# Attention with its maxima in a fused pre-LN block: seven PSUM banks shared by score and maximum products, each bank named in a fixed order, and most exponentials over one bank

## The chip, the cores and the metric

The kernel runs on one core of a Trainium2 chip, in one launch. The time is device microseconds from the first to the last instruction and what lies around them, the median of several runs. Engines are called as in the profile: PE (matrix products; PEld is its loading of weights), DVE (vector), ACT (activation), POOL, and SP, which issues most of the DMAs.

## The reference

S = 2048 rows, D = 512, 32 heads of 16. An attention block with a residual, then a gated MLP with a 2048x2048 mixing matrix and a residual. The change lies in the attention alone:

```
h  = x + attention(layernorm(x), wqkv, wo)
       scores = einsum("bhqd,bhkd->bhqk", q, k) * 16 ** -0.5
       p      = softmax(scores, axis=-1)
       o      = einsum("bhqk,bhkd->bhqd", p, v)
h2 = h + gmlp(layernorm(h), w_in, w_sp, b_sp, w_out)
```

## The kernel before

The kernel has four stages: layer norm and the projections to q, k and v; the attention; the first half of the MLP; the product with the mixing matrix and the output. The attention is worked in **units** (hg, qb, kb): four heads, 512 queries, 128 keys, 512 units in all. The loop takes two units per turn, and this text calls such a turn a **step**. What a step holds:

- Eight **score products** (L709), one per head and unit: 128 keys by 512 queries, contracted over 50 rows. A head is held in its own half of the rows of PE (t = 0 in rows 0 to 49, t = 1 in rows 64 to 113), so two products of different t can be in PE together. In the 50 rows are three pieces of q and k and two rows that subtract the row's maximum.
- Four **exponentials** (L715) on ACT, each over two banks of PSUM, 128x1024, into an SBUF tile `pt`.
- The **weighted sums** (L726), `pv`: four products of 32 columns side by side, over 512 queries (letter V) or over 256 (letter h, twice per unit).
- One **maximum step** for a group of queries eleven steps ahead: eight products over 48 rows (L235) into banks of their own. Six are read by a `reduce_max` on DVE (L240; letters M and m, four with t = 1 and two with t = 0). For the other two, keys were combined ahead: one (v) is read by an `abs` on ACT (L245), the other (u) by DVE, together with the result of that `abs` (L249).

The order on PE, ACT, DVE and SP is written by hand, as lists of letters that `play` reads (`ORDER` for six steps of eight, `FIRST_TWO` for the first two steps of 512 queries, `START` for the very first). An S in the list is a score product, and every second S issues the exponential too; a letter with a number is a product of the maximum step and the bank that it goes to. N, T and G set the ends of groups: negated maxima, their turning into rows, and the copy of the finished `pv` by ACT (L734). Semaphores are not written by hand: the tile framework puts a wait on an instruction where its tiles ask for one.

PSUM is cut into eight tiles of one bank (128x512 f32 each): `pv` one, `m0` to `m2` three (pool `ps_m`), and two tiles `s` of two banks (pool `ps_s`). A tile `s` gets two products and is read by one exponential; the two tiles alternate. Steps with maxima are those with n // 2 + 11 < 256, so 245 of them. In the last eleven, `FOUR` and plain code set the order, and a third tile `s` takes the place of the banks of the maxima.

## Time and profile before

| what | value |
|---|---|
| median of 3 runs | 1850.18 us (1849.63 to 1851.09) |
| profiled execution, span from first to last instruction | 1848.2 us |
| what lies around the span (median less span) | 2.0 us |
| ACT busy, `abs` in 300 to 1200 us | 186 times, so 186 steps in 900 us: 4.84 us each |
| PE's weight loads waiting for DVE to read a bank of maxima, 300 to 1300 us | 286.5 us, 568 times |
| granted PE clock | 1.00 in every stage but the end |

In the profile, a row of the view in order of time gives start, duration, engine, line, operation and tiles, then a count, and in brackets how long the engine had been idle and what ended that. Of PE two kinds of row are shown, its weight loads (PEld) and its matmuls; a matmul cannot start before its load, and it is the load that waits for a semaphore.

### The profile page before, as it was taken

How to read it: one execution, taken by the hardware profiler on the slowest of the kernel's cores; microseconds unless marked ns; L12 is line 12 of the kernel's file. 1: busy time of each engine (PE TensorE's matmuls, PEld its weight loads, DVE VectorE, ACT ScalarE, POOL GpSimd, SP SyncE). 2: the span in 40 equal slices, each digit the busy share in tenths (PEclk: the TensorE clock that was granted, in tenths of full speed). 3: DMA queues.
4: the chain of work that ended last, by engine and by line, in shares of the span. 5: the costliest groups of instructions: out<-in, count | busy, mean ns of one | idle time of the engine just before them, and what ended most of it. 6: DMA issues, size and time to landing. Idle time of an engine off the chain costs nothing.

```text
span 1848.2 us, 35986 instructions
## 1 busy us (share of the span) xinstructions
PE 1840.2 (100%) x13362; PEld 1028.3 (56%) x13362; DVE 1519.0 (82%) x3030; ACT 1363.4 (74%) x1696; POOL 225.7 (12%) x305
## 2 busy tenths in 40 slices
PE   9999999999999999999999999999999999999999
PEld 6875334433334333344333334343437889999998
DVE  6578999999999999999999999999936766877664
ACT  3325999999999999999999999999995444434221
POOL 2241000011010100000000000000001756001111
PEclk9999999999999999999999999999999999999999
DMA  6778111221120111022011012100124555768662
GB/s 195 198 193 193 42 25 31 55 47 29 39 57 18 53 39 25 17 50 39 14 39 38 19 30 49 25 14 14 31 55 124 165 162 170 224 189 272 200 195 91
DMA packets 148759, 160.15 MB, mean 87 GB/s; under 512 B 63096, under 2 KB 93320, under 8 KB 147240
## 3 DMA queue, kind: packets, MB, share of 16 engines
q1 hardware_dynamic: 143800, 146.44, 29.5%
q10 hardware_dynamic: 4752, 11.41, 1.6%
q8 instruction: 105, 1.72, 0.4%
q14 instruction: 70, 0.57, 0.1%
q0 software_dynamic: 32, 0.01, 0.0%
HBM read 101.26 MB, written 55.61 MB: 85 GB/s over the span
## 4 chain that ended last, share of the span: by engine, by line
PE 99%; DVE 0%; ACT 0%; issue 0%; DVEq 0%; ACTq 0%
PE pv L726 29%; PE m L235 22%; PE s L709 15%; PE acc L106 6%; PE acc L108 5%; PE acc L107 5%; PE g L108 4%; PE g L107 4%; PE g L106 4%; PE acc L644 2%; PE tp L1300 1%; PE acc L1321 0%; PE tp L996 0%; PE tp L389 0%; PE h L644 0%; PE acc L465 0%
## 5 line engine op out<-in xcount | busy, mean ns | idle before, releaser
L240 DVE TENSOR_REDUCE mx<-m 128x1 f32<-128x512 f32 x1508 | 948.5, 684 | 94.1 <-PE m L235 64.1
L715 ACT ACTIVATE pt<-s 128x1024 f32<-128x1024 f32 x1024 | 1012.5, 1024 | 12.6 <-PE m L235 6.6
L726 PE MATMUL pv<-pt,vst 128*32 128x256 f32 (+1 forms) x6048 | 590.5, 466 | 0.0
L235 PE MATMUL m<-kst,qst 48*128 48x512 f32 x1508 | 578.0, 468 | 0.1
L709 PE MATMUL s<-qst,kst 50*128 50x512 f32 x2048 | 568.1, 427 | 0.6 <-ACT pt L715 0.5
L235 PEld LDWEIGHTS m<-kst,qst 48*128 48x128 f32 x1508 | 236.7, 184 | 342.6 <-DVE mx L240 302.8
L709 PEld LDWEIGHTS s<-qst,kst 50*128 50x128 f32 x2048 | 273.5, 184 | 136.4 <-ACT pt L715 92.2
L726 PEld LDWEIGHTS pv<-pt,vst 128*32 128x32 f32 x6048 | 122.8, 108 | 227.5 <-issue 215.4
L235 PE MATMUL m<-uvs,qst 48*128 48x512 f32 x497 | 227.7, 458 | 0.0
L245 ACT ACTIVATE ab<-m 128x512 f32<-128x512 f32 x248 | 148.4, 598 | 76.5 <-PE m L235 76.4
L249 DVE CUSTOM_DVE_ANT_0 ab<-m,ab 128x512 f32<-128x512 f32 x249 | 169.4, 680 | 10.6 <-ACT pt L715 9.9
L100 POOL CAST mparts<-nm 128x16 fp32r<-128x16 f32 x32 | 6.3, 198 | 881.7 <-DVE nm L253 881.7
L235 PEld LDWEIGHTS m<-uvs,qst 48*128 48x128 f32 x497 | 90.8, 183 | 37.5 <-DVE mx L240 37.5
L936 ACT ACTIVATE ws<-a 128x512 fp32r<-128x512 f32 x80 | 45.7, 621 | 48.7 <-PE g L108 23.9
L1015 ACT ACTIVATE z<-acc 128x464 f32<-128x464 f32 (+2 forms) x64 | 27.6, 456 | 67.1 <-PE acc L108 67.1
L106 PE MATMUL acc<-wi,hT 128*128 128x464 f32 (+2 forms) x196 | 72.8, 371 | 0.0
L108 PE MATMUL acc<-wi,hT 128*128 128x464 f32 (+2 forms) x196 | 71.8, 366 | 0.0
L107 PE MATMUL acc<-wi,hT 128*128 128x464 f32 (+2 forms) x196 | 71.6, 365 | 0.0
L937 DVE TENSOR_TENSOR ws<-a,ws 128x512 fp32r<-128x512 f32 x80 | 56.3, 746 | 11.6 <-ACT ws L936 11.4
L98 ACT ACTIVATE part<-acc 128x512 fp32r<-128x512 f32 x32 | 19.1, 597 | 60.9 <-PE acc L108 51.6
L106 PE MATMUL g<-b,ws 128*128 128x344 f32 x192 | 62.6, 326 | 0.0
L936 ACT ACTIVATE ws<-s 128x512 fp32r<-128x512 f32 x32 | 19.5, 631 | 57.7 <-DVE s L956 57.7
(201 smaller groups left out, 2156.9 us busy)
## 6 DMA issues: line engine op xcount, KB each, us to landing
a<-in_w_sp SPq DMA_DIRECT2D x80, 256.0 KB
qst<-q_scr SPq DMA_DIRECT2D x192, 64.0 KB
z_scr<-z ACTq DMA_DIRECT2D x32, 344.0 KB
kst<-k_scr SPq DMA_DIRECT2D x42, 256.0 KB
k_scr<-part SPq DMA_DIRECT2D x16, 512.0 KB
q_scr<-part SPq DMA_DIRECT2D x16, 512.0 KB
z<-z_scr SPq DMA_DIRECT2D x14, 344.0 KB
b<-z_scr SPq DMA_DIRECT2D x24, 172.0 KB
```

Of the source, the lines that this page charges most:

```text
L106: nc.tensor.matmul(ps, lh, rh, start=first, stop=False)
L107: nc.tensor.matmul(ps, lh, rl, start=False, stop=False)
L108: nc.tensor.matmul(ps, ll, rh, start=False, stop=last)
L235: nc.tensor.matmul(acc, q[r, p, c], keys[r, p], start=True, stop=True)
L240: nc.vector.reduce_max(at(t, e if t else e - 1), acc, axis=AX.X)
L245: nc.scalar.activation(ab[0], acc, AF.Abs)
L249: nc.vector.tensor_tensor_reduce(ab[0], acc, ab[0], 0.5, LOW, ALU.add, ALU.max, at(0, 0))
L709: nc.tensor.matmul(s[:, t, :], k[r, p, kb * P:(kb + 1) * P], q[r, p, :], start=True, stop=True)
L715: nc.scalar.activation(t, s, AF.Exp, scale=DH ** -0.5)
L726: nc.tensor.matmul(pv[0][32 * j:32 * j + 32, cols], vst[hg % 2][:, c:c + 32], pts[j % 2][:, j // 2, cols], start=kb == 0, stop=kb == NB - ...
L936: nc.scalar.activation(hi, src, AF.Copy)
L937: (nc.gpsimd if el == "pool" else nc.vector).tensor_sub(lo, src, hi.bitcast(F32))
```

## The change

One pool `ps_s` now holds one tile `s` of four banks, for all steps with maxima. Banks 3 to 6 in the lists are the four banks of that tile, banks 0 to 2 are still `m0` to `m2`. Score products and maximum products both go to any of the seven. In the lists, `Sa5` is a score product with t = 0 into bank 5, whose exponential (128x512, that one bank) is issued with it; `Sb1` has t = 1. A small s only makes the product; the exponential then follows the next big S and covers both banks (128x1024), through a slice of the tile `s` with a step from bank to bank. In ORDER all eight are single; in FIRST_TWO, now one list for two steps, four exponentials cover two banks and eight one. `pt` becomes three tiles of four banks' width in place of six of two, the same bytes. After the steps with maxima, a pool `ps_d` with two tiles `s` of two banks takes the place of the one of before, so the last eleven steps are as they were. The products, their number and their operands stay.

```
+MB = 3
-ORDER = "v2 S S M1 N S h m0 S m1 M2 S S h S M0 u1 T S V M0".split()
+ORDER = "Sa5 M6 m3 M2 v4 Sb1 h Sb6 u0 M5 Sa4 h Sb2 m3 Sb6 Sa1 N M4 Sa0 V T".split()
-START = "S S m1 M0 S S h M2 v1 S S m0 S S M2 u1 V M0".split()
-FIRST_TWO = ["v2 S S M1 S h S m2 M0 h G M1 S S m2 S m0 S V".split(),
-             "u2 S S M1 m0 S S h h v2 M1 S S M0 S S M2 u1 V M0".split()]
+START = "Sa5 M6 m3 M2 v4 Sb1 f Sb6 u0 M5 Sa4 Sb2 m3 Sb6 Sa1 M4 Sa0 V".split()
+FIRST_TWO = ("sa6 Sb5 M2 sa4 m1 Sb3 h M0 m2 Sa6 sb5 h G M0 v1 M3 Sa6 Sb4 u2 V v1 M0 m3 Sb5 u6 Sb2 "
+             "h Sa4 M1 Sa0 M5 h Sb6 sa4 Sb3 m2 M1 Sa0 V").split()
...
-        pp = at.enter_context(tc.tile_pool(name="pp", bufs=6))
+        pp = at.enter_context(tc.tile_pool(name="pp", bufs=3))
         ps_v = at.enter_context(tc.tile_pool(name="ps_v", bufs=1, space=PSUM))
-        ps_s = at.enter_context(tc.tile_pool(name="ps_s", bufs=2, space=PSUM))
+        singles = at.enter_context(ExitStack())
+        ps_s = singles.enter_context(tc.tile_pool(name="ps_s", bufs=1, space=PSUM))
...
+        def product(out, hg, qb, kb, t, p):
+            r = slice(RG * t, RG * t + KM)
+            nc.tensor.matmul(out, kst[hg % 2][r, p, kb * P:(kb + 1) * P], qst[hg * NQ + qb][r, p, :],
+                             start=True, stop=True)
+        def exp(out, scores):
+            nc.scalar.activation(out, scores, AF.Exp, scale=DH ** -0.5)
...
             for x in order:
-                if x == "S":
-                    if opened:
-                        pts.append(opened.pop()())
...
+                if x[0] in "sS":
+                    if not open_:
+                        open_.extend([units.pop(0), new_pt(), {}])
+                    unit, pt, places = open_
+                    t, b = "ab".index(x[1]), int(x[2:])
+                    p = sum(u == t for u, _ in places)
+                    out = bank(b)
+                    product(out, *unit, t, p)
+                    places[t, p] = len(places)
+                    made.append((b, out, (t, p)))
+                    if x[0] == "s":
+                        continue
+                    made.sort(key=lambda m: m[0])
+                    k = len(places) - len(made)
...
+                    if len(made) == 1:
+                        exp(pt[:, k, :], out)
                     else:
...
+                        b0, b1 = (m[0] - MB for m in made)
+                        exp(pt[:, k:k + 2, :], four[0][:, b0:b1 + 1:b1 - b0, :])
...
+        four.append(ps_s.tile([P, 4, 512], F32, name="s"))
+        for b in range(4):
+            more[MB + b] = lambda b=b: four[0][:, b, :]
...
                 if not steps and not later:
                     maxima.close()
+                    singles.close()
+                    doubles.append(at.enter_context(tc.tile_pool(name="ps_d", bufs=2, space=PSUM)))
```

What this makes of PE's queue is seen in a step of ORDER, the same step in both kernels. A row names the line, the products' output and inputs, and in brackets the engine whose semaphore the instruction waits for before it starts (`Activation_49` is ACT, `DVE_49` is DVE). First before, on PE, from the product v2 to m1; `s` is the tile of scores, `m` a bank of maxima, `pv` the weighted sum:

```order
L235 MATMUL m_10724<-uvs_106,qst 128x512
L709 MATMUL s<-qst,kst_105 128x512 [waits Activation_49]
L709 MATMUL s<-qst,kst_105 128x512
L235 MATMUL m_10733<-kst_105,qst 128x512 [waits DVE_49]
L709 MATMUL s<-qst,kst_105 128x512 [waits Activation_49]
L726 MATMUL pv<-pt,vst_103 32x256 x4
L235 MATMUL m_10742<-kst_105,qst 128x512 [waits DVE_49]
L709 MATMUL s<-qst,kst_105 128x512
L235 MATMUL m_10748<-kst_105,qst 128x512 [waits DVE_49]
```

Score products go to `s` alone and wait for ACT, one per tile of two banks; products into `m` wait for their reader. Now the same step after the change, on PE, from M2 to the second Sb6 of the list (M2, v4, Sb1, h, Sb6, u0, M5, Sa4, h, Sb2, m3, Sb6); L700 are score products, L236 products of the maximum step, and `s` is the tile of banks 3 to 6:

```order
L236 MATMUL m_10143<-kst_105,qst 128x512
L236 MATMUL s<-uvs_106,qst 128x512 [waits DVE_49]
L700 MATMUL m_10149<-qst,kst_105 128x512
L725 MATMUL pv<-pt,vst_103 32x256 x4
L700 MATMUL s<-qst,kst_105 128x512 [waits Activation_49]
L236 MATMUL m_10158<-uvs_106,qst 128x512
L236 MATMUL s<-kst_105,qst 128x512 [waits Activation_49]
L700 MATMUL s<-qst,kst_105 128x512 [waits DVE_49]
L725 MATMUL pv<-pt,vst_103 32x256 x4
L700 MATMUL m_10170<-qst,kst_105 128x512
L236 MATMUL s<-kst_105,qst 128x512 [waits Activation_49]
L700 MATMUL s<-qst,kst_105 128x512 [waits DVE_49]
```

Score and maximum products now alternate in the tile `s`; each of the six products into it carries a wait, and none of the four into `m` banks does in this stretch. The second place is FIRST_TWO, after the change, on PE (m2, Sa6 and sb5, h, M0, v1, M3, Sa6, Sb4, u2, V):

```order
L236 MATMUL m_10209<-kst_105,qst 128x512 [waits DVE_49]
L700 MATMUL s<-qst,kst_105 128x512 [waits Activation_49] x2
L725 MATMUL pv<-pt,vst_103 32x256 x4
L236 MATMUL m_10231<-kst_105,qst 128x512 [waits DVE_49]
L236 MATMUL m_10234<-uvs_106,qst 128x512
L236 MATMUL s<-kst_105,qst 128x512
L700 MATMUL s<-qst,kst_105 128x512 [waits DVE_49]
L700 MATMUL s<-qst,kst_105 128x512 [waits Activation_49]
L236 MATMUL m_10244<-uvs_106,qst 128x512
L725 MATMUL pv<-pt,vst_103 32x512 [waits PE_49]
```

Here half a weighted sum and the products M0 and v1 stand between sb5 and M3, and a whole weighted sum follows on Sb4 and u2; the products into `s` keep their waits except M3, ahead of which nothing has read `s` since sb5 was let in.

More of the change, by code (lines that the diff above doesn't have):

```diff
@@ L686, in block_kernel, with new_pt, score, weigh @@
         fixed(kst[1])
-        pp = at.enter_context(tc.tile_pool(name="pp", bufs=6))
+        pp = at.enter_context(tc.tile_pool(name="pp", bufs=3))
         ps_v = at.enter_context(tc.tile_pool(name="ps_v", bufs=1, space=PSUM))
-        ps_s = at.enter_context(tc.tile_pool(name="ps_s", bufs=2, space=PSUM))
+        singles = at.enter_context(ExitStack())
+        ps_s = singles.enter_context(tc.tile_pool(name="ps_s", bufs=1, space=PSUM))
         pv = {}
-        def score(*unit):
-            first, second = scores_of(*unit)
-            first()
-            return second()
-        def scores_of(hg, qb, kb, p):
-            q, k = qst[hg * NQ + qb], kst[hg % 2]
+        def new_pt():
+            return pp.tile([P, 4, 512], F32, name="pt")
+        def product(out, hg, qb, kb, t, p):
[4 more added lines that the diff above has]
+            nc.scalar.activation(out, scores, AF.Exp, scale=DH ** -0.5)
+        def score(unit, p, pt):
             turn[0] += len(later)
-            pool = later[0] if later and turn[0] % 3 == 2 else ps_s
+            pool = later[0] if turn[0] % 3 == 2 else doubles[0]
             s = pool.tile([P, 2, 512], F32, name="s")
-            def product(t):
-                r = slice(RG * t, RG * t + KM)
-                nc.tensor.matmul(s[:, t, :], k[r, p, kb * P:(kb + 1) * P], q[r, p, :],
-                                 start=True, stop=True)
             def second():
-                product(1)
-                t = pp.tile([P, 2, 512], F32, name="pt")
-                nc.scalar.activation(t, s, AF.Exp, scale=DH ** -0.5)
-                return t
-            return lambda: product(0), second
-        def weigh(hg, qb, kb, pts, cols=slice(0, 512)):
-            if kb == 0:
+                product(s[:, 1, :], *unit, 1, p)
+                exp(pt[:, 2 * p:2 * p + 2, :], s)
+            return lambda: product(s[:, 0, :], *unit, 0, p), second
+        def weigh(unit, pt, places, cols=slice(0, 512)):
+            hg, qb, kb = unit
+            if kb == 0 and cols.start == 0:
                 pv[0] = ps_v.tile([P, 512], F32, name="pv")
@@ L726, in weigh @@
                 nc.tensor.matmul(pv[0][32 * j:32 * j + 32, cols], vst[hg % 2][:, c:c + 32],
-                                 pts[j % 2][:, j // 2, cols], start=kb == 0,
+                                 pt[:, places[j // 2, j % 2], cols], start=kb == 0,
                                  stop=kb == NB - 1 and cols.stop == 512)
+        PLACES = {(t, p): 2 * p + t for t in range(2) for p in range(2)}
         def gather(hg, qb, pool=sm):
@@ L747, in gather, with play @@
             sums_[0] = (hg, cols, sums, pool)
-        def play(order, prev, unit):
-            hg, qb, *kbs = unit
+        def play(order, units):
             ending = pending[:]
@@ L754, in play @@
             ends.clear()
-            halves = [slice(0, 256), slice(256, 512)]
-            opened, pts = [], []
+            units = list(units)
+            open_, made = [], []
             for x in order:
-                if x == "S":
-                    if opened:
-                        pts.append(opened.pop()())
-                    else:
-                        k, p = divmod(len(pts), 2)
-                        first, second = scores_of(hg, qb, kbs[k], p)
-                        first()
-                        opened.append(second)
-                elif x == "h":
-                    cols = halves.pop(0)
-                    if prev is not None:
-                        weigh(*prev, cols)
-                    elif halves:
-                        pv[0] = ps_v.tile([P, 512], F32, name="pv")
-                        for j in range(4):
-                            nc.tensor.matmul(pv[0][32 * j:32 * j + 32, :], vst[0][:, :32],
-                                             vst[0][:, :512], start=True, stop=True)
+                if x[0] in "sS":
[12 more added lines that the diff above has]
+                    k = len(places) - len(made)
+                    for i, (_, _, head_) in enumerate(made):
+                        places[head_] = k + i
+                    if len(made) == 1:
+                        exp(pt[:, k, :], out)
+                    else:
+                        b0, b1 = (m[0] - MB for m in made)
+                        exp(pt[:, k:k + 2, :], four[0][:, b0:b1 + 1:b1 - b0, :])
+                    made.clear()
+                    if len(places) == 4:
+                        waiting.append([tuple(open_), 0])
+                        open_.clear()
+                elif x == "h":
+                    h = waiting[0][1]
+                    weigh(*waiting[0][0], slice(256 * h, 256 * h + 256))
+                    waiting[0][1] += 1
+                    if h:
+                        done[0] = waiting.pop(0)[0][0]
@@ L776, in play @@
                 elif x == "V":
-                    weigh(hg, qb, kbs[0], pts[:2])
+                    done[0] = waiting[0][0][0]
+                    weigh(*waiting.pop(0)[0])
                 elif x == "G":
-                    gather(*prev[:2])
+                    gather(*done[0][:2])
+                elif x == "f":
+                    pv[0] = ps_v.tile([P, 512], F32, name="pv")
+                    for j in range(4):
+                        nc.tensor.matmul(pv[0][32 * j:32 * j + 32, :], vst[0][:, :32],
+                                         vst[0][:, :512], start=True, stop=True)
@@ L785, in play @@
                         max_rows()
-                    elif kbs[0] == 6 and sums_:
+                    elif done[0] is not None and done[0][2] == 5 and sums_:
                         invert()
@@ L789, in play, with play_four @@
                     steps_of[x[0]].pop(0)(int(x[1:]))
-            assert not ending and len(pts) == 4
-            played.append(pts[2:])
-        def play_four(at, prev):
-            waiting, opened = [prev], []
+            assert not ending and not open_ and not units and not made
+        waiting, done, four, doubles = [], [None], [], []
+        def play_four(units):
+            opened, unit = [], None
             for x in FOUR:
@@ L798, in play_four @@
                     if opened:
-                        pts = waiting[-1][-1]
-                        pts.append(opened.pop()())
-                    else:
-                        if waiting[-1] is prev or len(waiting[-1][-1]) == 2:
-                            waiting.append((*at.pop(0), []))
-                        unit = waiting[-1]
-                        first, second = scores_of(*unit[:3], len(unit[-1]))
+                        opened.pop()()
+                        if p:
+                            waiting.append([(unit, pt, PLACES), 0])
+                            unit = None
+                    else:
+                        if unit is None:
+                            unit, pt, p = units.pop(0), new_pt(), -1
+                        p += 1
+                        first, second = score(unit, p, pt)
                         first()
@@ L808, in play_four @@
                 elif x == "V":
-                    unit = waiting.pop(0)
-                    weigh(*unit)
-                    if unit[2] == NB - 1:
-                        gather(*unit[:2])
+                    unit_ = waiting.pop(0)[0]
+                    weigh(*unit_)
+                    if unit_[0][2] == NB - 1:
+                        gather(*unit_[0][:2])
                 else:
                     more_h(1)
-            return waiting.pop()
         played, pending = [], []
@@ L858, in block_kernel @@
         units = [(hg, qb, kb) for hg in range(HG) for qb in range(NQ) for kb in range(NB)]
-        prev, turn, later = None, [2], []
+        turn, later = [2], []
+        four.append(ps_s.tile([P, 4, 512], F32, name="s"))
+        for b in range(4):
+            more[MB + b] = lambda b=b: four[0][:, b, :]
         with tc.manual_schedule(engines={E.PE, E.Activation, E.DVE, E.SP}):
             for n in range(0, len(units), 2):
-                (hg, qb, kb), (_, _, kb1) = units[n:n + 2]
+                hg, qb, kb = units[n]
                 if hg + 1 < HG and n % 64 < 24 and n % 4 == 0:
@@ L880, in block_kernel @@
                 if steps:
-                    play(START if not n else FIRST_TWO[place] if place < 2 < n else ORDER, prev, (hg, qb, kb, kb1))
-                    pts1 = played.pop()
+                    if place or not n:
+                        if place != 1 or n == 2:
+                            play(ORDER if n else START, units[n:n + 2])
+                    else:
+                        play(FIRST_TWO, units[n:n + 4])
                 elif n % 4 == 0:
@@ L885, in block_kernel @@
                         load_o(h_rows[3])
-                    prev = play_four(units[n:n + 4], prev)
+                    play_four(units[n:n + 4])
                 elif n < 492:
@@ L889, in block_kernel @@
                         pending.pop()()
-                    pts = [score(hg, qb, kb, 0), score(hg, qb, kb, 1)]
-                    weigh(*prev)
-                    pts1 = [score(hg, qb, kb1, 0), score(hg, qb, kb1, 1)]
-                    more_h(4)
-                    weigh(hg, qb, kb, pts)
+                    for i in range(2):
+                        pt = new_pt()
+                        for p in range(2):
+                            for step in score(units[n + i], p, pt):
+                                step()
+                        if i:
+                            more_h(4)
+                        weigh(*waiting.pop(0)[0])
+                        waiting.append([(units[n + i], pt, PLACES), 0])
                     if turned:
                         max_rows()
-                if steps or n == 490:
-                    prev = (hg, qb, kb1, pts1)
                 if kb == 6 and sums_:
@@ L906, in block_kernel @@
                     split_o(h_rows[0], "pool", "pool")
-            weigh(*prev)
-            gather(*prev[:2], e2)
+            done[0] = waiting[0][0][0]
+            weigh(*waiting.pop(0)[0])
+            gather(*done[0][:2], e2)
     attn.close()
```

## The prediction

> **What bounds the kernel now.** I first asked for busy time by stretch of the attention, to see which engine is full, and then for the groups of lines in 300 to 1200 us.

> ```profile
> core 0: us, PE busy (x) PEld busy (x) DVE busy (x) ACT busy (x) POOL busy (x), PEclk, DMA share, GB/s
> 500.00:700.00 200.00, 199.74 (x1656) 79.60 (x1654) 183.11 (x348) 185.85 (x213) 12.83 (x23) 1.00 0.17 39
> ```

> ```profile
> L240 DVE TENSOR_REDUCE mx<-m 128x1 f32<-128x512 f32 x1116 | 701.5, 684 | 68.1 <-PE m L235 46.0 <-PE s L709 16.4
> ...
> L245 ACT ACTIVATE ab<-m 128x512 f32<-128x512 f32 x186 | 111.3, 598 | 55.1 <-PE m L235 54.9
> ```

> DVE is busy 183 of 200 us and ACT 186, and neither is full. PE's 199.74 is the busy time of overlapping matmuls and no measure. One `abs` is made per step, so a step lasts 900 / 186 = 4.84 us. The view of waits between 300 and 1300 us says who holds whom:

> ```profile
> PEld m L235 <- DVE mx L240: 286.5, 568, 0.8
> ...
> PEld s L709 <- ACT pt L715: 73.9, 175, 0.7
> ACT ab L245 <- PE m L235: 61.1, 179, 0.4
> DVE mx L240 <- PE m L235: 51.3, 225, 0.3
> ```

> PE waits for DVE or ACT to read a bank, and these wait for PE's next product. The three engines run in a ring, each nearly full, and the ring goes through the banks. What it lives on is that PE writes one bank while another is being read. In the view in order of time (start, duration):

> ```profile
> 703.08 1.29 DVE L240 TENSOR_REDUCE mx<-m 128x1 f32<-128x512 f32 x2 [0.27 <-PE m L235]
> 703.11 0.60 ACT L245 ACTIVATE ab<-m 128x512 f32<-128x512 f32 x1 [0.34 <-PE m L235]
> 703.12 0.39 PE L235 MATMUL m<-kst,qst 48*128 48x512 f32 x1
> 703.12 0.39 PE L709 MATMUL s<-qst,kst 50*128 50x512 f32 x1
> ```

> At 703.12 us two products run while DVE reads a second bank and ACT a third.

> **The change: seven banks, but a wait for the whole tile.** On paper each product waits for the last reader of its own bank. The order rows say otherwise. In ORDER, bank 6 is read by DVE (M6), and the first Sb6 into it waits for ACT alone: ACT has just read v4, in bank 4. Sa4 goes into bank 4, last read by ACT, and waits for DVE, which has just read M5 in bank 5. The second m3 goes where DVE read, and waits for ACT (Sa4's exponential); the second Sb6 goes where ACT read, and waits for DVE (that m3). In each of these four the engine that is waited for is the one that read the previous product into `s`, whatever its bank. Products into `m0` to `m2`, tiles of their own, show no such wait. So I take it that the four banks of `s` are one thing to the semaphores: a product into `s` starts when the one before has been read, and they pass one at a time. PE's queue is in order, so behind a waiting product stand the `m` products and the weighted sums, and behind those ACT and DVE. This ends the overlap seen above.

> The price of one passage is load after release, matmul, wait of the reader, and reading. Its parts in the trace of before:

> ```profile
> 702.54 0.50 PE L235 MATMUL m<-kst,qst 48*128 48x512 f32 x1
> 702.55 0.50 PE L235 MATMUL m<-uvs,qst 48*128 48x512 f32 x1
> ...
> 704.42 0.19 PEld L235 LDWEIGHTS m<-kst,qst 48*128 48x128 f32 x2 [0.22 <-DVE mx L240]
> ```

> ```profile
> 704.65 1.02 ACT L715 ACTIVATE pt<-s 128x1024 f32<-128x1024 f32 x1
> ...
> 704.76 0.41 PE L709 MATMUL s<-qst,kst 50*128 50x512 f32 x2
> ```

> ```profile
> 705.16 0.68 DVE L240 TENSOR_REDUCE mx<-m 128x1 f32<-128x512 f32 x1
> ```

> ```profile
> 705.10 0.64 PE L726 MATMUL pv<-pt,vst 128*32 128x256 f32 x8
> ...
> 705.72 0.18 PEld L709 LDWEIGHTS s<-qst,kst 50*128 50x128 f32 x1 [0.46 <-ACT pt L715]
> 705.72 0.50 PE L709 MATMUL s<-qst,kst 50*128 50x512 f32 x1
> ...
> 706.07 0.40 PE L709 MATMUL s<-qst,kst 50*128 50x512 f32 x1
> ...
> 706.39 1.07 PE L726 MATMUL pv<-pt,vst 128*32 128x512 f32 x8
> ```

> - ACT's reading ends at 704.65 + 1.02 = 705.67 and the load that waits starts at 705.72: 0.05. From DVE it is the same (703.08 + 1.29 = 704.37, load at 704.42).
> - A product that has waited takes 0.50 to its end, load included.
> - The products of 702.54 and 702.55 end at 703.04 and 703.05; DVE starts at 703.08 and ACT at 703.11: 0.04 and 0.06.
> - Reading takes 0.68 on DVE, 0.60 on ACT for one bank (the `abs`; I take it for an exponential over one bank too, of which there is no row), 1.02 for two.

> A passage is thus 0.05 + 0.50 + 0.06 + 0.60 = **1.21 us** through ACT, 0.05 + 0.50 + 0.04 + 0.68 = **1.27** through DVE, and 1.63 through an exponential over two banks.

> *A step of ORDER* has ten products into `s`: Sa5, v4, Sb6, Sa4, Sb6 are read by ACT, M6, m3, M5, m3, M4 by DVE. That is 5 x 1.21 + 5 x 1.27 = 12.40 us. Work on the `m` banks and the halves of the weighted sum lie beside a reading or a wait. The whole sum V does not quite: before, a product ends at 706.07 + 0.40 = 706.47, and the first after V starts and ends here:

> ```profile
> 707.39 0.50 PE L235 MATMUL m<-kst,qst 48*128 48x512 f32 x1
> ```

> From 706.47 to 707.89 are 1.42 us, against the 1.27 of the passage through M4, so V adds 0.15: 12.55.

> *The two steps of FIRST_TWO* have four exponentials over two banks, five single ones (Sa6, Sb4, Sb5, Sa4, Sb6) and four readings by DVE (M3, m3, u6, M5): 4 x 1.63 + 5 x 1.21 + 4 x 1.27 = 17.65 us. Between sb5 and M3 stand half a sum and M0. From the product that ends at 704.76 + 0.41 = 705.17 over a half sum to the end of the next at 706.22 are 1.05 us, and M0's reading comes ahead of M3's on DVE. So after Sa6's exponential: 0.55 for sb5, 1.05 to M0, 0.04 and 0.60 for its reading (the start-to-start of DVE: 1.29 for two), 0.68 for M3's, together 2.92 in place of 1.27, so 1.65 more. In the same way from Sb4 over V, with M0 ahead of m3: 1.42 + 0.64 + 0.68 = 2.74 in place of 0.66 + 1.27, so 0.8 more. With 0.15 for the last V it is 20.25.

> Eight steps come to 6 x 12.55 + 20.25 = 95.6 us, 11.94 a step, and 7.10 more than now. Times 245 steps: **+1740 us**. Against the profiled execution, 1848.2 + 1740 = 3588; with the 2.0 us around its span, **3590**.

> **What the other edits cost.** Eight exponentials over one bank for four over two are more work for ACT. The rows above start an exponential at 703.61 behind the `abs` of 703.11, and eight in a row before the end of the stage give the longer one:

> ```profile
> 703.61 1.02 ACT L715 ACTIVATE pt<-s 128x1024 f32<-128x1024 f32 x1
> ...
> 1379.45 7.44 ACT L715 ACTIVATE pt<-s 128x1024 f32<-128x1024 f32 x8 [0.19 <-PE s L709]
> ```

> Back to back, one bank costs 0.50 and two (7.44 - 1.02) / 7 = 0.92: 8 x 0.50 - 4 x 0.92 = 0.32 a step more. In a step of 12 us, of which ACT works some 5, this is hidden; it would be paid only if the passages did not wait for each other. Three `pt` in place of six halves delay an exponential at most until the sum of three units earlier, far back at this pace: nothing. The loads of k, q and v on SP's queue are as many and now have over twice the time; the dense stages before and after, and the last eleven steps with their two tiles of two banks, are as before: nothing.

> **Bounds.** 0.05 more or less per passage, on (6 x 10 + 13) / 8 = 9.1 passages a step, moves the time by 112 us. Without the delays in FIRST_TWO it is 78 us less. If at every second passage of ORDER a reading of an `m` bank stood 0.25 us in the way, it would be 10 / 2 x 0.25 x 0.75 x 245 = 230 more. Together about 3400 to 3930, and the ends need all of it at once: 3450 to 3900.

> **Rivals.**

> ```profile
> L734 ACT ACTIVATE o<-pv 128x512 f32<-128x512 f32 x30 | 17.8, 592 | 0.0
> ```

> *Each product waits for its own bank alone* (the change then does what it says). Place: PE's loads in ORDER. For it speaks that PE and the readers work in different banks at one time in the trace of before; against it the four waits on the wrong engine. PE would run ahead, and ACT would be the bound: nine readings of 0.50 and an eighth of the copy of `pv`, 4.57 a step, 0.27 less than now: 1850 - 66 = 1784, faster. It decides when a product into `s` starts before the last one into `s` has been read. [...]

> *The same, but ACT doesn't run back to back*: nine readings at 0.60, 5.47 a step, 0.63 more: 2004.

> *PE's clock falls.* PE would stand still for half of each passage. The first products of the program show what a slow PE costs, 634 ns for most and 413 for the last:

> ```profile
> L465 PE MATMUL acc<-idle x14: 413/634/634, 1.2 to 6.7; 128*128 128x512 bf16 x14
> ```

> ```profile
> 8.25 2.48 PE L441 MATMUL acc<-wv,xT 128*128 128x512 f32 x8 [0.69 <-ACT xT L98]
> 11.69 0.55 PE L389 MATMUL tp<-ident,xg 128*128 128x128 f32 x3 [0.95 <-ACT xg L378]
> ```

> ```profile
> 8.00:12.00 4.00, 2.77 (x11) 1.66 (x12) 3.48 (x12) 2.05 (x4) 4.00 (x6) 1.00 0.95 342
> ```

> At 0.22 more on each of 9.1 passages, 245 steps give +490: 4080. Against it: the pauses are some 0.7 us, of the size of those in the first stage (0.69 and 0.95 us idle ahead of a product), where the granted clock is 1.00 (third from the end in the row of 8 to 12 us). [...]

> **How the numbers follow.** My forecast has 0.79, 4080 has 0.10, 1784 has 0.06, 2004 has 0.03, and 0.02 is left for what I have not thought of. 3450 to 3900 then holds 0.8. A measurement here can tell 0.2% from no change. Faster is the first rival (0.06), the same 0.01, slower 0.93.

> **What would show it.** By step: 245 steps of about 12 us between two `abs`, and some 20 for the two of FIRST_TWO together; ACT busy near 5 of 12 us and DVE near 4.5; behind each reading of `s` a PE load 0.05 us later, also where the bank is another; waits of PE's loads for ACT and DVE at the head of the list, well over 1000 us together; granted clock 1.00, products near 0.50 us. It is wrong if PE writes one bank of `s` while another is read, or if a step is under 5 us. A clock below 1, with products above 0.6 us, would show the third rival.

## The result and the profile after

After the change the kernel takes **4613.48 us** (median of 4 runs, 4611.26 to 4613.8), before it 1849.96 us (4 runs, 1849.63 to 1851.09): 2.493 times as long (95% interval 2.490 to 2.497). The forecast was 3590 us, its range ended at 3900. The profiled execution has a span of 4612.0 us.

The busy time by stretch, in the 200 us shown of before (busy us and instructions of PE, PEld, DVE, ACT and POOL, then granted clock, DMA share, GB/s):

```profile
500.00:700.00 200.00, 142.02 (x502) 42.74 (x498) 58.81 (x103) 65.12 (x108) 4.32 (x8) 0.50 0.03 8
```

DVE and ACT work a third of the time, where they worked nine tenths. That they would work far less was expected (some 4.5 and 5 of 12 us). What was not: the third figure from the end, ahead of the DMA share, is 0.50. The page's row of the granted clock, in 40 equal slices, shows that this holds nearly throughout:

```profile
PEclk9755555555555555555555555555555555569999
```

The clock is at 0.50 of full speed as long as the steps with maxima last, and at 1.00 ahead of them (100 to 160 us) and in the dense stages behind (4120 to 4200 us). The waits between 300 and 1300 us (total, times, longest):

```profile
DVE mx L241 <- PE s L236: 311.3, 147, 3.4
ACT pt L704 <- PE s L700: 278.4, 141, 2.5
...
PEld s L236 <- ACT pt L704: 182.9, 155, 1.2
PEld s L700 <- DVE mx L241: 153.7, 116, 1.7
```

Readers wait for products into `s`, and products into `s` for readers: L236, a product of maxima, for ACT's exponential, and L700, a score product, for DVE's maximum, both ways round. In order of time, one step of ORDER on PE; the products into `s` from v4 to the next v4, and the weighted sums between them (start, duration):

```profile
1009.64 0.79 PE L236 MATMUL s<-uvs,qst 48*128 48x512 f32 x1 [0.78 <-DVE mx L241]
...
1010.37 1.08 PE L725 MATMUL pv<-pt,vst 128*32 128x256 f32 x8
1011.38 0.79 PE L700 MATMUL s<-qst,kst 50*128 50x512 f32 x1
...
1012.86 0.79 PE L236 MATMUL s<-kst,qst 48*128 48x512 f32 x1 [0.69 <-ACT pt L704]
1014.43 0.79 PE L700 MATMUL s<-qst,kst 50*128 50x512 f32 x1 [0.78 <-DVE mx L241]
...
1015.15 1.08 PE L725 MATMUL pv<-pt,vst 128*32 128x256 f32 x8
...
1016.16 0.79 PE L236 MATMUL s<-kst,qst 48*128 48x512 f32 x1
1017.77 0.79 PE L700 MATMUL s<-qst,kst 50*128 50x512 f32 x1 [0.82 <-DVE mx L241]
...
1019.24 0.79 PE L236 MATMUL s<-kst,qst 48*128 48x512 f32 x1 [0.68 <-ACT pt L704]
...
1019.97 1.93 PE L725 MATMUL pv<-pt,vst 128*32 128x512 f32 x8
1021.83 0.79 PE L700 MATMUL s<-qst,kst 50*128 50x512 f32 x1
1023.31 0.79 PE L236 MATMUL s<-kst,qst 48*128 48x512 f32 x1 [0.69 <-ACT pt L704]
1024.88 0.79 PE L236 MATMUL s<-kst,qst 48*128 48x512 f32 x1 [0.78 <-DVE mx L241]
...
1026.45 0.79 PE L236 MATMUL s<-uvs,qst 48*128 48x512 f32 x1 [0.78 <-DVE mx L241]
```

Ten passages, one at a time, as forecast; but the step lasts 1026.45 - 1009.64 = 16.81 us instead of 12.55, and each product 0.79 us instead of 0.50. Start to start, a passage is 1.47 or 1.48 through ACT, 1.57 to 1.61 through DVE, 1.73 or 1.74 with half a weighted sum behind the product (v4 and Sa4), and 2.59 with the whole sum (M4). Inside one passage, that of Sb6 from 1011.38:

```profile
1012.21 0.60 ACT L704 ACTIVATE pt<-s 128x512 f32<-128x512 f32 x1 [0.65 <-PE m L236]
...
1012.86 0.28 PEld L236 LDWEIGHTS s<-kst,qst 48*128 48x128 f32 x1 [1.19 <-ACT pt L704]
```

The product ends at 1011.38 + 0.79 = 1012.17, ACT starts 0.04 later and ends at 1012.81, and the next load comes 0.05 later. Of the four parts three are as forecast. Only the product has changed, by 0.29.

### The profile page after: what moved, and what is told of

It is laid out like the page before. It is cut to its first block, busy times and chain, and to the rows that moved or that the text cites. A ratio compares the mean times of both kernels' runs of the same rounds, so it can differ in the third digit from the quotient of the medians.

```text
span 4612.0 us, 35874 instructions
## 1 busy us (share of the span) xinstructions
PE 3456.1 (75%) x13362; PEld 1406.3 (30%) x13362; DVE 1605.2 (35%) x3030; ACT 1528.4 (33%) x2556; POOL 225.4 (5%) x305
## 5 line engine op out<-in xcount | busy, mean ns | idle before, releaser
L241 DVE TENSOR_REDUCE mx<-s 128x1 f32<-128x512 f32 x1015 | 701.6, 691 | 1830.0 <-PE s L236 1234.2
L236 PE MATMUL s<-kst,qst 48*128 48x512 f32 x1015 | 791.4, 780 | 533.1 <-ACT pt L704 388.1
L704 ACT ACTIVATE pt<-s 128x512 f32<-128x512 f32 (+1 forms) x1054 | 695.2, 664 | 1492.3 <-PE s L700 1092.2
L700 PE MATMUL s<-qst,kst 50*128 50x512 f32 x1218 | 834.6, 763 | 450.7 <-DVE mx L241 354.5
L725 PE MATMUL pv<-pt,vst 128*32 128x256 f32 (+1 forms) x6048 | 1025.5, 771 | 0.0
L700 PEld LDWEIGHTS s<-qst,kst 50*128 50x128 f32 x1218 | 303.4, 278 | 1328.4 <-DVE mx L241 609.1
L700 PE MATMUL m<-qst,kst 50*128 50x512 f32 x830 | 647.1, 780 | 0.0
L704 ACT ACTIVATE pt<-m 128x512 f32<-128x512 f32 x830 | 493.4, 594 | 327.2 <-PE s L236 220.7
L236 PEld LDWEIGHTS s<-kst,qst 48*128 48x128 f32 x1015 | 291.6, 287 | 929.5 <-ACT pt L704 691.5
L241 DVE TENSOR_REDUCE mx<-m 128x1 f32<-128x512 f32 x493 | 331.5, 686 | 387.1 <-PE m L236 386.6
L250 DVE CUSTOM_DVE_ANT_0 ab<-m,ab 128x512 f32<-128x512 f32 x219 | 151.5, 692 | 491.1 <-PE m L236 406.5
L236 PE MATMUL m<-kst,qst 48*128 48x512 f32 x493 | 308.5, 724 | 0.0
L236 PE MATMUL s<-uvs,qst 48*128 48x512 f32 x215 | 169.9, 790 | 164.5 <-DVE mx L241 144.0
L700 PEld LDWEIGHTS m<-qst,kst 50*128 50x128 f32 x830 | 238.8, 288 | 152.0 <-issue 149.1
L725 PEld LDWEIGHTS pv<-pt,vst 128*32 128x32 f32 x6048 | 150.8, 138 | 343.0 <-issue 342.1
L236 PE MATMUL m<-uvs,qst 48*128 48x512 f32 x282 | 220.8, 783 | 0.0
L236 PEld LDWEIGHTS s<-uvs,qst 48*128 48x128 f32 x215 | 61.2, 285 | 273.4 <-DVE mx L241 237.6
L236 PEld LDWEIGHTS m<-kst,qst 48*128 48x128 f32 x493 | 121.1, 288 | 53.9 <-issue 51.5
L236 PEld LDWEIGHTS m<-uvs,qst 48*128 48x128 f32 x282 | 79.1, 280 | 49.9 <-issue 49.9
```

The lines of the kernel that those rows point to most:

```text
L236: nc.tensor.matmul(acc, q[r, p, c], keys[r, p], start=True, stop=True)
L241: nc.vector.reduce_max(at(t, e if t else e - 1), acc, axis=AX.X)
L250: nc.vector.tensor_tensor_reduce(ab[0], acc, ab[0], 0.5, LOW, ALU.add, ALU.max, at(0, 0))
L700: nc.tensor.matmul(out, kst[hg % 2][r, p, kb * P:(kb + 1) * P], qst[hg * NQ + qb][r, p, :], start=True, stop=True)
L704: nc.scalar.activation(out, scores, AF.Exp, scale=DH ** -0.5)
L725: nc.tensor.matmul(pv[0][32 * j:32 * j + 32, cols], vst[hg % 2][:, c:c + 32], pt[:, places[j // 2, j % 2], cols], start=kb == 0, stop=kb = ...
```

## The experiments

Two questions were put. Is the tile of four banks the cause, rather than the lists or the single exponentials? And what holds the clock at 0.50, and how much of the time is it worth? In the diffs, line numbers move, so L713, L247, L717, L254, L263 and L738 in the later runs are L700, L236, L704, L241, L250 and L725 of the changed kernel. The kernel before took 1850.06 us beside the first four runs, 1850.57 beside the next three, 1849.92 and 1850.42 beside the last.

### Four tiles of one bank

```
-        four.append(ps_s.tile([P, 4, 512], F32, name="s"))
+        four.extend(ps_s.tile([P, 512], F32, name=f"s{b}") for b in range(4))
         for b in range(4):
-            more[MB + b] = lambda b=b: four[0][:, b, :]
+            more[MB + b] = lambda b=b: four[b]
```

and the small s in FIRST_TWO made large, since an exponential cannot cover two tiles.

> The changed kernel with its banks 3 to 6 as four tiles of one bank each in place of one tile of four; lists and all else as they are, but the four exponentials over two banks in FIRST_TWO become eight over one. Theory (the wait for the whole tile is the loss, and the slow PE clock follows from it): a step of 4.6 to 4.85 us, granted clock 1.00, 1780 to 1850 us. Rival A (exponentials over one bank, or the new orders themselves, cost): a step above 5.4 us, 2000 us or more, whatever the tiles are. Rival B (the clock falls by itself with this order of products): clock 0.50 in the steps, over 2500 us.

Measured: **1828.83 us** (4 runs, 1828.49 to 1829.36), against 1850.06 of before (7 runs): 0.9885 (0.9869 to 0.9902), so 21 us faster than before and 2785 us faster than the change. In order of time:

```profile
1008.18 0.59 ACT L704 ACTIVATE pt<-s 128x512 f32<-128x512 f32 x1
1008.33 0.68 DVE L241 TENSOR_REDUCE mx<-s 128x1 f32<-128x512 f32 x1
...
1008.62 0.50 PE L700 MATMUL s<-qst,kst 50*128 50x512 f32 x1
```

At 1008.62 the next product into banks 3 to 6 starts, while ACT still reads one of them (to 1008.77) and DVE another (to 1009.01). In the step of the changed kernel above, no product into these banks starts before the last reading has ended. Busy time by stretch, and one long row of exponentials:

```profile
500.00:700.00 200.00, 198.62 (x1686) 81.39 (x1683) 184.00 (x353) 192.57 (x385) 12.69 (x21) 1.00 0.19 41
```

```profile
1002.53 3.08 ACT L704 ACTIVATE pt<-s 128x512 f32<-128x512 f32 x6
```

ACT is busy 192.57 of 200 us, and (3.08 - 0.60) / 5 = 0.50 us is the price of an exponential over one bank back to back. So this is the first rival of the prediction, which gave 1784 us for it: ACT is nearly full, with some 4% of its time left.

### The kernel before, with its score tiles cut from one

The lists, the two-bank exponentials and the `m` banks stay as before; only the two tiles `s` become halves of one tile of four banks.

```
+        four, side = [ps_s.tile([P, 4, 512], F32, name="s")], [0]
...
-            pool = later[0] if later and turn[0] % 3 == 2 else ps_s
-            s = pool.tile([P, 2, 512], F32, name="s")
+            if later and turn[0] % 3 == 2:
+                s = later[0].tile([P, 2, 512], F32, name="s")
+            else:
+                side[0] ^= 2
+                s = four[0][:, side[0]:side[0] + 2, :]
```

> The kernel before, with its old lists and exponentials over two banks; only its two tiles of scores of two banks are cut out of one tile of four banks. Theory (the framework passes products one reader at a time through a tile): four exponentials a step in a row, 4 x 1.63 = 6.5 us and with the weighted sums up to 7.9 a step, 2250 to 2600 us at a clock of 1.00, more if the clock falls. Rival A (the lists or the single exponentials are to blame, not the tile): 1850, no change.

Measured: 3228.8 us (one run), mean clock 0.689. One declaration makes the old order 1379 us slower, so neither the lists nor the single exponentials are needed for the loss. The time lies above the figure for full clock, and here too the clock falls; how much of the miss that is was not worked out. In short stretches one sees it go up and down:

```profile
274.10:277.40 3.30, 2.12 (x18) 0.72 (x14) 1.37 (x3) 1.51 (x2) 0.00 (x0) 1.00 0.00 0
277.50:284.20 6.70, 5.57 (x28) 1.81 (x27) 3.17 (x7) 2.98 (x3) 0.00 (x0) 0.50 0.02 3
284.40:287.60 3.20, 2.07 (x16) 0.64 (x13) 1.37 (x3) 1.53 (x3) 0.00 (x0) 1.00 0.03 2
```

### Two tiles of two banks

```
-        four.append(ps_s.tile([P, 4, 512], F32, name="s"))
+        four.extend(ps_s.tile([P, 2, 512], F32, name=f"s{b}") for b in range(2))
         for b in range(4):
-            more[MB + b] = lambda b=b: four[0][:, b, :]
+            more[MB + b] = lambda b=b: four[b // 2][:, b % 2, :]
```

> The changed kernel with banks 3 to 6 as two tiles of two banks (3 and 4, 5 and 6); all else as it is. In ORDER the ten products into these banks fall in five pairs that follow each other in one tile. Theory: one wait per pair is left, so at least 5 x 1.24 = 6.2 us a step, with the weighted sums up to 8.6; 2180 to 2770 us at a clock of 1.00, a third more above 1850 (2300 to 3100) at 0.50. Rival A: as the whole change, above 3500. Which clock this gets, with PE busy near half the time, is open.

Measured: 3597.99 us (one run), mean clock 0.606: 1015 us less than one tile, above both ranges of the theory and inside the rival's, which was anything above 3500. In the stretches below the clock is 0.50 but for 3 us at a time:

```profile
557.10:560.30 3.20, 2.44 (x20) 0.92 (x16) 1.56 (x3) 1.56 (x4) 0.00 (x0) 1.00 0.00 0
560.50:652.50 92.00, 74.05 (x304) 22.39 (x304) 35.56 (x65) 38.26 (x67) 0.47 (x3) 0.50 0.10 22
```

The direction fits the theory of the tile, four tiles 1829, two 3598, one 4613, and two tiles are not as slow as one. The size does not fit what was made of it: at half clock two chains were thought to lie beside each other to a larger part. Why they do so little was not taken apart.

### Useless products in one half of the rows

Behind each product into `s` stand two more, of 48 rows in one half of PE's rows, into bank 0, whose own products go to bank 1. Nobody reads them.

```
+            for _ in range(2):
+                nc.tensor.matmul(filler[0], k[:KS, p, :P], q[:KS, p, :], start=True, stop=True)
```

> The changed kernel, with two more products of 48 rows by 512 columns on PE behind each product into the tile of four banks, into a bank of their own that nobody reads (bank 0; its other products go to bank 1). They are work of no use; the waits stay. Theory (a PE that stands still for half the time gets half the clock): granted clock 1.00 again, products that have waited 0.50 us in place of 0.79, 3600 to 4050 us, so faster than the changed kernel with more work done. Rival (the clock is low for another reason, for instance products in one row half at a time): clock stays 0.50 and the time is above 4613, up to 5600 us with twenty products of 0.43 us a step in the queue.

Measured: 5458.15 us, mean clock 0.561. The stretch of 1000 to 1200 us:

```profile
1000.00:1200.00 200.00, 189.10 (x611) 82.76 (x610) 48.85 (x85) 55.43 (x90) 1.51 (x4) 0.50 0.03 6
```

PE is busy 189 of 200 us and the clock is still 0.50. So in this run a PE that hardly pauses was not enough to bring the clock back: the length of its pauses, by which the prediction weighed this rival, does not settle the clock here.

### Useless products over all rows

The same places, less those where a weighted sum comes before the next product into `s`, with operands of ones over 128 rows; bank 0's own products again go to bank 1. Three kernels: three or four of 128 rows, and as the control four of 48 rows.

```
+                nxt = [y[0] in "hVf" for y in order[i + 1:] if y[0] in "hVf" or y[0] in "sSMmvu" and int(y[-1]) >= MB]
+                filling[0] = bool(nxt) and not nxt[0]
...
+            for _ in range(FILL):
+                nc.tensor.matmul(filler[0], filler[1][:ROWS, :P], filler[1][:ROWS], start=True, stop=True)
```

> The changed kernel with three useless products of 128 rows by 512 columns behind each product into the tile of four banks, except where a weighted sum comes before the next such product; they go to bank 0, whose own products use bank 1. The useless products multiply ones and nobody reads them. Theory: the clock follows the share of the whole array that is at work, rows counted, and not the share of time in which TensorE is busy. A step at half clock then has about 0.98 of the array's time filled (8 x 3 x 0.43 + 10 x 0.43 x 0.4 + 3.4 us in about 17.5 us), so the clock returns to 1.00, and at 1.00 about 0.6 to 0.7 stays filled: the clock is at 1.00 for most of the time and the run takes 3500 to 4000 us, less than the 4613 us of the changed kernel although it does more work. Rival (the clock is held down by something that more work on TensorE does not change, such as its waits on other engines): the clock stays at 0.50 and the time is 4650 to 5200 us.

> As the run with three, with four useless products of 128 rows. Theory (share of the array): the clock at 1.00 for at least as much of the time as with three, and 3500 to 4000 us, since at 1.00 four products of 0.21 us lie inside the 1.2 us of a passage. Rival: 0.50, and 5000 to 5500 us, since at 0.50 four of 0.43 us no longer fit into a passage.

> The control: four useless products at the same places, of 48 rows instead of 128. In time they fill TensorE as the four of 128 rows do, in rows they fill 0.375 of that. Theory (share of the array): about 0.55 of the array's time filled at half clock, as in the run with two useless products of 48 rows; the clock stays at 0.50 and the time is 5000 to 5700 us. Rival (what counts is the time in which TensorE is busy, and two useless products were too few or stood at the wrong places): this run has the same clock as the one with four products of 128 rows.

Measured: three of 128 rows 4481.09 us at a mean clock of 0.901, four of 128 rows 4495.94 at 0.974, four of 48 rows 5848.24 at 0.543. The stretch of 1000 to 1200 us, of the kernel with four of 128 rows first:

```profile
1000.00:1200.00 200.00, 178.72 (x830) 61.84 (x846) 60.84 (x107) 68.76 (x111) 5.39 (x8) 0.96 0.05 14
```

and of that with four of 48 rows, in whose one execution the stages ahead and behind had 0.85 in place of 1.00:

```profile
1000.00:1200.00 200.00, 190.76 (x641) 70.93 (x637) 45.35 (x79) 51.96 (x84) 5.92 (x6) 0.50 0.06 11
```

The same number of products at the same places; the kernel whose PE is busy for more of the time has the lower clock. What differs is the rows of the useless products, 128 or 48, and with them the clock, 0.96 or 0.50. It came out as the theory had it, in all three, though its filling for three products adds up to 15.4 of 17.5 us, 0.88 and not 0.98. (Its 0.43 us per product at half clock is seen in the run with two: two useless products take 1.22 us, one product 0.79.) The times did not: 5848 us lies above the 5000 to 5700 expected, 4481 and 4496 us far above the 3500 to 4000, and these two little below the change, though the clock was near 1. Either the forecast's sum for full clock was wrong, or the useless products cost time themselves. The trace of the run with three showed Sa0, now in bank 1, waiting behind Sa1's exponential in that bank, and V behind Sa0: 2.60 us from M4 to the next product into the tile, 1003.99 to 1006.59.

### The sum at full clock

The products of bank 0 were spread over banks 1 and 2, with three useless products of 128 rows as above, and then without any:

```
-ORDER = "Sa5 M6 m3 M2 v4 Sb1 h Sb6 u0 M5 Sa4 h Sb2 m3 Sb6 Sa1 N M4 Sa0 V T".split()
+ORDER = "Sa5 M6 m3 M2 v4 Sb1 h Sb6 u2 M5 Sa4 h Sb1 m3 Sb6 Sa2 N M4 Sa1 V T".split()
```

> As the run with three useless products of 128 rows, but the products that stood in bank 0 are spread over banks 1 and 2, so that none of them waits for a reading that has just begun (in the run before, the one named Sa0 stood in bank 1 behind Sa1 and held the weighted sum V and the next product into the tile for 2.60 us in place of some 1.4). This measures a step at full clock with the lists of the change. Theory (passages are as long as predicted at full clock, and the half clock is most of what the prediction missed): a step at a granted clock of 1.00 lasts 12.6 to 13.2 us. Rival (the prediction's sum is wrong at any clock): a step at 1.00 stays above 14 us. The whole run, at a mean clock near 0.90 as before: 4050 to 4350 us by the theory, near 4480 by the rival.

> The same lists without any useless product: the control for the spread over two banks. Nothing but bank names of products outside the tile differs from the changed kernel, so both theories expect a granted clock of 0.50 through the attention and 4600 to 4640 us; a time further off would mean that the spread itself costs or saves something.

Measured: with useless products 4135.38 us at a mean clock of 0.959; without them 4748.74 at 0.570, and here the stretch reads

```profile
500.00:700.00 200.00, 137.98 (x480) 41.23 (x479) 57.58 (x101) 62.25 (x105) 4.32 (x8) 0.50 0.02 6
```

With equal lists, useless work makes the kernel 613 us *faster*. The control itself came out 109 us above the 4600 to 4640 expected: its steps of ORDER are as in the change (16.83 us), the rest is in FIRST_TWO, where the products of bank 0 still went to bank 1 alone. From v4 to v4, on PE, without useless products:

```profile
1003.86 0.79 PE L247 MATMUL s<-uvs,qst 48*128 48x512 f32 x1 [0.78 <-DVE mx L254]
...
1020.69 0.79 PE L247 MATMUL s<-uvs,qst 48*128 48x512 f32 x1 [0.78 <-DVE mx L254]
```

With them, the steps of ORDER at full clock were 13.40 us, above the 13.2 of the theory and below the 14 of the rival. In the trace of that run the useless products behind Sb6 held u2 back to 1025.36 us, when M5's product came too, and DVE read u2 first:

```profile
1025.36 0.49 PE L247 MATMUL m<-uvs,qst 48*128 48x512 f32 x1
1025.37 0.50 PE L247 MATMUL s<-kst,qst 48*128 48x512 f32 x1
...
1026.00 0.69 DVE L263 CUSTOM_DVE_ANT_0 ab<-m,ab 128x512 f32<-128x512 f32 x1 [1.88 <-PE s L247]
...
1026.62 0.69 DVE L254 TENSOR_REDUCE mx<-s 128x1 f32<-128x512 f32 x1
1027.36 0.50 PE L713 MATMUL s<-qst,kst 50*128 50x512 f32 x1 [0.74 <-DVE mx L254]
```

M5's passage is 1.99 us. So one more run leaves out the three useless products at that place (`"hVf"` becomes `"hVfu"` in the rule above).

> The run with three useless products of 128 rows and the spread over two banks, less the three that stood between Sb6 and u2 in a step of ORDER. There they held u2 back until M5's product came, so that DVE read u2 first and M5's passage was 1.99 us instead of some 1.27. Theory (the prediction's sum for a step is right at full clock, and all but some 0.2 us of what it missed is the half clock): a step of ORDER at a granted clock of 1.00 lasts 12.5 to 12.9 us, against 13.40 in the run before. Rival (the passage through M5 is long for a reason of its own, or the shorter filling lets the clock fall for good): steps stay at 13.2 us or more, or none runs at 1.00. The whole run: 3900 to 4100 us if the clock stays near 0.95 in the mean, up to 4500 us if it falls to 0.50 for half of the time.

Measured: 4205.06 us at a mean clock of 0.888, and a step of ORDER inside the expected 12.5 to 12.9. The whole is above the 3900 to 4100 expected for a clock near 0.95 and below the 4500 for 0.50 half of the time; its clock lies between. Two steps on end, from one u2 to the next, by stretch, and the readings by DVE that bound them:

```profile
1044.30:1057.00 12.70, 11.90 (x58) 3.97 (x58) 5.01 (x10) 5.19 (x10) 0.00 (x0) 1.00 0.02 2
1057.00:1069.70 12.70, 11.91 (x58) 3.98 (x58) 4.86 (x9) 5.18 (x10) 0.00 (x0) 1.00 0.00 0
```

```profile
1044.32 0.69 DVE L263 CUSTOM_DVE_ANT_0 ab<-m,ab 128x512 f32<-128x512 f32 x1 [0.74 <-PE m L247]
...
1057.00 0.69 DVE L263 CUSTOM_DVE_ANT_0 ab<-m,ab 128x512 f32<-128x512 f32 x1 [0.74 <-PE m L247]
...
1069.69 0.69 DVE L263 CUSTOM_DVE_ANT_0 ab<-m,ab 128x512 f32<-128x512 f32 x1 [0.75 <-PE m L247]
```

At a granted clock of 1.00 a step lasts 12.68 and 12.69 us. Its passages, on PE:

```profile
1057.51 0.49 PE L247 MATMUL s<-kst,qst 48*128 48x512 f32 x1 [0.69 <-ACT pt L717]
...
1058.78 0.50 PE L713 MATMUL s<-qst,kst 50*128 50x512 f32 x1
...
1059.96 0.49 PE L247 MATMUL s<-kst,qst 48*128 48x512 f32 x1
...
1061.24 0.50 PE L713 MATMUL s<-qst,kst 50*128 50x512 f32 x1
...
1062.43 0.49 PE L247 MATMUL s<-kst,qst 48*128 48x512 f32 x1
...
1063.08 1.07 PE L738 MATMUL pv<-pt,vst 128*32 128x512 f32 x8
1064.08 0.50 PE L713 MATMUL s<-qst,kst 50*128 50x512 f32 x1
```

M5 1.27, Sa4 1.18, m3 1.28, Sb6 1.19, M4 with V behind it 1.65.

## Why the prediction was wrong

**The whole-tile wait: right.** Products into different banks of `s` pass one at a time, and the cut of the tile decides: the same bank lists take 4613 us with one tile and 1829 with four (where, too, four pairs of exponentials became single ones), and the old lists go from 1850 to 3229 us when their two tiles become one. The prediction's reading of the waits on the wrong engine was the right one.

**The passage and the step of ORDER at full clock: right.** 1.21 and 1.27 us were forecast, 1.18 to 1.19 and 1.27 to 1.28 measured. The step was forecast at 12.55 and lasts 12.69. The small misses cancel in part: five passages through ACT are some 0.1 shorter together, and V adds 0.38 to M4's passage and not 0.15.

**The step that failed: the clock.** The rival "PE's clock falls" was given a chance of 0.10, argued from the length of the pauses, and it is what happened. Two runs settle its weight: the same list takes 16.83 us a step at 0.50 without the useless products and 12.69 at 1.00 with them. So of the 4.26 us that a step of ORDER took beyond the forecast, some 4.1 are the clock; the useless products, which only add work, can hardly have shortened the step.

**Its size failed as well.** 0.22 us on each of 9.1 passages gave 4080. By the trace of the change, a step of ORDER has:

| passages of a step | forecast | at 0.50 | more |
|---|---|---|---|
| 3 through ACT, nothing behind (Sb6, Sb6, Sa5) | 1.21 | 1.48 | 0.8 |
| 4 through DVE (M5, m3, M6, m3) | 1.27 | 1.57 to 1.61 | 1.2 |
| 2 through ACT, half a sum behind (v4, Sa4) | 1.21 | 1.74 | 1.1 |
| 1 through DVE, V behind (M4) | 1.42 | 2.59 | 1.2 |

At half clock a product that waited takes 0.79, load included, so 0.29 and not 0.22. And at half clock the weighted sums (1.08 and 1.93 us in place of 0.64 and 1.07) are no longer covered by a reading: they came into the chain, which the price of the rival left out. The last two rows alone are half of the excess. The 0.22 itself came from the program's first products, for which the view by stretch gives a granted clock of 1.00 (0 to 8 us): no row of before shows a product at half clock.

**FIRST_TWO** was forecast at 20.25 us. In the trace of the change eight steps repeat every 128.83 us, which leaves 128.83 - 6 x 16.81 = 27.97 for these two. Together the excess is (6 x 4.26 + 7.72) / 8 x 245 = 1019 us, and 4613 - 3590 = 1023. How much of the 7.72 is the clock was not measured for these lists. The two runs with bank 0 spread out, equal in their lists, give a hint. From the `abs` of the last step of ORDER ahead of FIRST_TWO to that of the first step behind it are 41.91 us at 1.00 with useless products (1063.70 to 1105.61) and 49.18 at 0.50 without them (1088.82 to 1138.00); less the one step of ORDER in this, FIRST_TWO takes 28.5 and 32.4. There full clock saves 3.8 us, net of what the useless products cost. No run shows the 20.25 of the forecast at full clock; whether its sum for FIRST_TWO also fell short, or the products moved to bank 1 and the useless ones took the rest, stays open. (In the forecast's bounds, the delays in FIRST_TWO of 1.65 and 0.8 us come to 75 us by its own terms and not 78, which changes nothing.)

**Why the argument against the rival misled.** It took PE's pauses of 0.69 and 0.95 us in the first stage, where the clock was 1.00, as the standard. Those products have 128 rows; here the products that wait have 48 or 50, in one half of the array, and in the step shown 12 of 16 score and maximum products start together with another (within 0.01 us), where in a step before all 16 do. The run with two useless products of half the rows shows the clock at 0.50 with PE busy 95% of the time, and the pair with four shows 0.96 at 89% with 128 rows and 0.50 at 95% with 48. Nor are the pauses of the changed kernel much longer than those of the first stage: the longest of the step shown is 0.82 us, and the longest of 300 to 1300 us 1.1 us, at a clock of 0.50. In the run of before with one tile the clock goes up and down, 1.00 for 3.3 us and 0.50 for the next 6.7, while that of the changed kernel stays at 0.50. Why the clock falls with such pauses and such products was not shown.

**Rival 1** (own-bank waits) was priced at 1784 us. With four tiles it is 1829: ACT is the fullest engine, as the price had it, but its time is not quite filled (192.57 of 200 us).

## What to carry to other kernels

Look at how a buffer is declared before you count its parts: one tile of four banks was one thing to wait for, whatever bank each product names, and cutting it into four tiles turned a loss of 2764 us into a gain of 21. When a change thins out PE's work, price a slower clock too (here 0.50 in place of 1.00), for everything that PE does in the new chain, also what was covered before (here a whole weighted sum, 1.93 us in place of 1.07). And do not infer the clock from PE's busy time or pauses alone (here 0.50 at 95% busy, 0.96 at 89%): compare the stage with one that has the same shapes.
